# Making the two fp16 parts of a group's row maxima directly behind its last maxima

## The chip, the cores and the metric

The kernel runs on one core of a Trainium2 chip. The metric is the device time of one execution in microseconds (us). Engines are named as in the profile: PE is TensorE (matrix products and transposes), PEld its weight loads, DVE is VectorE, ACT is ScalarE, POOL is GpSimd, and SP is SyncE, which only issues DMAs here. Each engine takes its instructions in a fixed order and waits for the other engines by semaphores.

## The reference

Four layers work on a sequence of 2048 tokens of width 640, in the order A, B, A, B, each on the layer-normed stream and added back to it. A is linear attention with 32 heads of width 20. B is an attention in 4 segments of 512 tokens, with a memory of the segments before. The part that matters here is the softmax inside a segment of B:

```python
for s in range(N):                               # N = 4 segments, L = 512 tokens each
    qs, ks, vs = q[:, :, s], k[:, :, s], v[:, :, s]
    logits = einsum("bhqd,bhkd->bhqk", qs, ks) * scale + mask     # causal, 512 x 512 for each head
    p = softmax(logits, axis=-1)
    a_dot = einsum("bhqk,bhkd->bhqd", p, vs)
    a_mem = (phi(qs) @ M) / (phi(qs) @ z + 1e-6)
    o = g * a_mem + (1 - g) * a_dot
    M, z = M + phi(ks).T @ vs, z + phi(ks).sum()
```

## The kernel before

**Groups.** The 32 heads of a segment are done in 8 groups of 4 heads (two partition halves `par`, two heads `p` in each), so the two B layers have 2 x 4 x 8 = 64 groups. I number them 0 to 63 in the order of time. For each group the kernel does:

- `row_max`: the logits with the query rows on the partitions, 2 banks of PSUM per call (matmul L687); DVE reduces each block to the maximum of each query row under the causal mask (L694, a custom instruction that is followed by a read of its accumulator into a column of `mg`). A group has 16 of these, in five calls, `max` 0 to 4.
- The maxima as two fp16 rows: `m2` holds a high and a low part of `-mg / 2^14`, made by two DVE instructions (L703, L704) on 128 x 16 numbers. PE transposes `m2` (L707), ACT copies the 32 x 128 result out of PSUM (L709), and SP writes it by two small DMAs (L712) into the last rows of `qs`, so that the score matmul subtracts the maxima by itself.
- `scores`: the logits a second time, transposed (L724), exp on ACT (L728), the causal corner on POOL (L735).
- `weigh`: the weighted sum of `v` (L751, 16 steps in one bank), and `normalize`.

**The order of the work.** Two streams are woven together: the attention of one segment's groups, and the dense work of the next segment (projections L311 and L325, transposes L268, memory reads L370, output projections). The attention is given out in short bursts, three per group (`STRETCHES`), and dense work stands between the bursts. A burst works on three groups at once, written as "back" 0, 1 or 2: the new one, the one before, and the one before that. The first burst of a round holds the last scores of the oldest group, the first two calls of maxima of the new group, and then, for the group whose maxima were finished in the burst before, `rows`: `m2`, its transpose and the copies. The `sum` steps stand behind it.

**What sets each engine's order.** PE takes its instructions in the order in which the program was written (`MANUAL = ("PE",)`). For DVE, ACT, POOL and SP a scheduler orders the instructions: of those that it thinks ready it takes the one that was written first. So an instruction that is written later can be overtaken on DVE by others that are written earlier and are ready by then. All PSUM tiles share eight banks.

## Time and profile before

| | before |
|---|---|
| median of 3 runs | 1851.29 us (1851.12 to 1856.78) |
| the profiled execution | 1850.11 us, span 1848.4 us |
| PE busy | 1716.3 us, 93% of the span |
| DVE busy | 1144.3 us, 62% |
| ACT busy | 911.4 us, 49% |
| POOL busy | 503.3 us, 27% |
| granted PE clock, mean | 0.994 |
| L707, the transposes of `m2` | 64, of about 0.23 us |
| L703 and L704, the two parts | 64 each, of about 0.17 us |

The span is the time from the first to the last instruction of the profiled execution; the execution's own time is 1.7 us more. "Idle before" in brackets behind a row is how long the engine stood still ahead of that instruction, and behind the arrow is what ended the wait. The granted clock is 1.00 or 0.50 in any short stretch. Busy times of PE are spans of pipelined matmuls, so they say where PE was held up rather than how full it was. Where rows on one engine overlap, the next instruction has started before the last one's result was out.

### The profile page before, as it was taken

To read this page: it belongs to the slowest core of one execution; us is meant where nothing else is said; L and a number is where in the kernel's file an instruction comes from. 1 tells how busy PE (TensorE), PEld (TensorE's weight loads), DVE (VectorE), ACT (ScalarE), POOL (GpSimd) and SP (SyncE) were. 2 spreads that over 40 slices of the span, in tenths; PEclk is the share of its full clock that TensorE was granted. 3 is DMA by queue.
4 is the path that set the end of the run, shared out by engine and by line. 5 is a ranking of instruction groups with operands and counts; after the bars stand their busy time and mean duration, and the time that the engine had idled before them with its cause. 6 is when DMAs were issued, how large, how long until landed. Compare 5 with 4: busy or idle time off the path is not lost.

```text
span 1848.4 us, 36154 instructions
## 1 busy us (share of the span) xinstructions
PE 1716.3 (93%) x13032; PEld 1071.0 (58%) x13032; DVE 1144.3 (62%) x3890; ACT 911.4 (49%) x1696; POOL 503.3 (27%) x925
## 2 busy tenths in 40 slices
PE   6999999998999998898989999999989889898998
PEld 4666676654654565454556776756446546544555
DVE  7655353677767686766663421527677677677883
ACT  5455433266555545545554433333664665455553
POOL 1534430022122112224344334200221231232331
PEclk9999999999999999999999999999999999999999
DMA  7442443312222331351212112332122222223332
GB/s 253 157 183 89 158 151 107 107 52 88 78 65 87 109 98 59 112 192 65 70 55 86 51 33 92 133 115 90 55 86 91 85 90 89 94 76 105 121 111 87
DMA packets 123307, 185.96 MB, mean 101 GB/s; under 512 B 13676, under 2 KB 85484, under 8 KB 120952
## 3 DMA queue, kind: packets, MB, share of 16 engines
q1 hardware_dynamic: 109416, 137.44, 23.2%
q0 software_dynamic: 4496, 25.23, 3.8%
q10 hardware_dynamic: 9216, 20.98, 3.0%
q8 instruction: 103, 1.69, 0.4%
q14 instruction: 76, 0.62, 0.1%
HBM read 104.41 MB, written 78.64 MB: 99 GB/s over the span
## 4 chain that ended last, share of the span: by engine, by line
PE 73%; DVE 12%; ACT 6%; issue 4%; POOL 2%; DMA 2%; SPq 1%; POOLq 0%; ACTq 0%; DVEq 0%
PE ps L325 31%; PE ps L311 18%; PE ps L751 7%; DVE junk L694 5%; PE ps L268 4%; ACT pe L728 3%; PE ps L370 3%; PE ps L724 3%; PE ps L452 2%; PE ps L687 2%; POOL e L341 1%; PE ps L582 1%; PE ps L764 1%; DVE nat L547 1%; DVE st L286 1%
## 5 line engine op out<-in xcount | busy, mean ns | idle before, releaser
L694 DVE CUSTOM_DVE_ANT_0 junk<-ps,maskw 128x512 bf16<-128x512 f32 (+3 forms) x1024 | 499.3, 488 | 83.2 <-PE ps L687 27.0
L728 ACT ACTIVATE pe<-ps,lsc 128x512 f32<-128x512 f32 x640 | 392.6, 691 | 172.6 <-PE ps L724 170.6
L735 POOL TENSOR_SCALAR_AFFINE_SELECT pe<-pe 128x256 f32<-128x256 f32 (+1 forms) x640 | 234.2, 372 | 694.4 <-ACT pe L728 689.5
L325 PEld LDWEIGHTS <-xT 128*128 128x128 f16 x2880 | 281.8, 99 | 125.4 <-issue 19.4
L325 PEld LDWEIGHTS <-oT 128*128 128x128 f16 x1920 | 186.4, 98 | 78.7 <-issue 7.6
L341 POOL TENSOR_SCALAR e<-e 128x320 f32<-128x320 f32 (+1 forms) x104 | 163.8, 1575 | 163.2 <-ACT e L337 154.4
L751 PE MATMUL ps<-pe,v 128*32 128x512 f32 (+3 forms) x2048 | 159.4, 447 | 13.5 <-ACT pe L728 6.6
L724 PE MATMUL ps<-qs,ks 62*128 62x384 f16 (+3 forms) x1024 | 131.6, 299 | 33.8 <-DVE mg L694 22.8
L325 PE MATMUL ps<-w_Bv,xT 128*128 128x320 f16 x960 | 142.4, 302 | 1.9 <-DVE mg L694 1.9
L325 PE MATMUL ps<-w_Bo,oT 128*128 128x320 f16 x960 | 141.2, 299 | 2.6 <-DVE mg L694 1.4
L325 PE MATMUL ps<-w_Av,xT 128*128 128x320 f16 x960 | 140.8, 304 | 1.6 <-DVE w_Av L234 1.0
L311 PE MATMUL ps<-xT,w_Bq 128*128 128x512 f16 x600 | 139.5, 379 | 1.5 <-DVE mg L694 0.9
L311 PE MATMUL ps<-xT,w_Bk 128*128 128x512 f16 x600 | 139.5, 379 | 0.2 <-DVE xn L391 0.2
L325 PE MATMUL ps<-w_Ao,oT 128*128 128x320 f16 x960 | 139.5, 299 | 0.0
L311 PE MATMUL ps<-xT,w_Aq 128*128 128x512 f16 x600 | 136.0, 379 | 1.3 <-DVE xT L273 0.9
L325 PE MATMUL ps<-w_Ak,xT 128*128 128x320 f16 x960 | 135.6, 299 | 1.4 <-DVE mg L694 1.4
L348 ACT ACTIVATE v<-ps 128x320 f32<-128x320 f32 x128 | 55.5, 436 | 143.4 <-PE ps L325 139.1
L291 POOL TENSOR_TENSOR rs<-rs,mhalf 128x1 f32<-128x1 f32 x64 | 35.3, 552 | 302.7 <-DVE rs L290 302.4
L751 PEld LDWEIGHTS ps<-pe,v 128*32 128x32 f32 x2048 | 66.5, 112 | 82.8 <-issue 69.3
L687 PE MATMUL ps<-ks,qs 60*128 60x512 f16 (+3 forms) x1024 | 108.4, 297 | 5.5 <-ACT pe L728 3.4
L547 DVE SCALAR_TENSOR_TENSOR nat<-ps,nat 128x512 f16<-128x512 f32 x80 | 55.3, 691 | 89.9 <-ACT nat L546 87.5
L273 DVE TENSOR_TENSOR xT<-ps,xT 128x384 f16<-128x384 f32 (+1 forms) x128 | 60.3, 484 | 78.3 <-ACT xT L272 78.1
(151 smaller groups left out, 2228.5 us busy)
## 6 DMA issues: line engine op xcount, KB each, us to landing
x<-xn ACTq DMA_DIRECT2D x48, 320.0 KB
qs<-qd SPq DMA_DIRECT2D x128, 120.0 KB
ks<-kd SPq DMA_DIRECT2D x128, 120.0 KB
xo<-x SPq DMA_DIRECT2D x48, 320.0 KB
pqd<-pq POOLq DMA_DIRECT2D x40, 256.0 KB, 2.5
pqi<-pqd SPq DMA_DIRECT2D x32, 320.0 KB
qd<-nat SPq DMA_DIRECT2D x40, 256.0 KB
kd<-nat SPq DMA_DIRECT2D x40, 256.0 KB
```

The lines of the kernel that those rows point to most:

```text
L268: nc.tensor.transpose(pt[:, (c - c0) * P:(c - c0 + 1) * P], src[:, c * P:(c + 1) * P], self.ident)
L273: nc.vector.tensor_tensor(dst[:, c0:c1, 1, i * P:(i + 1) * P], v, hi, op=OP.subtract)
L311: nc.tensor.matmul(p, w[:, c, a, t * P:(t + 1) * P], xT[:, c, b, :], start=k == 0, stop=k == 3 * C - 1)
L325: nc.tensor.matmul(p, xT[:, c, a, i * P:(i + 1) * P], w[:, c, b, n * HN:(n + 1) * HN], start=k == 0, stop=k == 3 * C - 1)
L341: nc.gpsimd.tensor_scalar(e, e, 1.0, eps, op0=OP.min, op1=OP.add)
L547: nc.vector.scalar_tensor_tensor(nat[:, 1], p, QK_SHIFT, nat[:, 0], op0=OP.mult, op1=OP.subtract)
L687: nc.tensor.matmul(bs[par][:, a:a + n], qs[r, p, i * P:(i + 1) * P], ks[r, p, :n], start=True, stop=True)
L694: nc.vector.tensor_tensor_reduce(junk[:, :n], bs[par][:, a:a + n], self.maskw[:, SEG - n:], 1.0, NEG, OP.add, OP.max, G["mg"][:, par, p, i ...
L724: nc.tensor.matmul(b[:, a:a + n], ks[r, p, j * P:(j + 1) * P], qs[r, p, j * P:], start=True, stop=True)
L728: nc.scalar.activation(e, b, AF.Exp, scale=self.lsc)
L735: nc.gpsimd.affine_select(d, d, pattern=pat, compare_op=OP.is_ge, fill=0.0, base=0, channel_multiplier=-1)
L751: nc.tensor.matmul(G["pv"][32 * h4:32 * h4 + 32, j * P:], v[j][:, h * E1:h * E1 + 32], G.pop((p, par, j)), start=j == 0, stop=j == 2, skip ...
```

## The change

The two DVE instructions that make `m2` leave `max_rows` and get a method of their own, `split_max`. It is called from a new entry `split` in the third burst, directly behind the group's last call of maxima. The transpose, the copy and the two DMAs stay where they were, in the first burst of the next round, behind the first two calls of maxima of the next group. No instruction is added or removed.

```diff
-             [("exp", 2, 1), ("exp", 3, 1), ("max", 4, 0), ("load", 0, 0)]]
+             [("exp", 2, 1), ("exp", 3, 1), ("max", 4, 0), ("split", 0, 0), ("load", 0, 0)]]
...
-    def max_rows(self, G):
+    def split_max(self, G):
-        nc, bp, qs = self.nc, self.bp, G["qs"]
+        nc, bp = self.nc, self.bp
         mg = G["mg"].rearrange("q a p i -> q a (p i)")
         m2 = bp.tile([P, 2, 2, 2 * NT], F16, tag="m2", name="m2", bufs=2)
         nc.vector.tensor_scalar(m2[:, :, 0], mg, -1.0 / M_ONE, None, op0=OP.mult)
         nc.vector.scalar_tensor_tensor(m2[:, :, 1], mg, -1.0 / M_ONE, m2[:, :, 0],
                                        op0=OP.mult, op1=OP.subtract)
+        G["m2"] = m2
+
+    def max_rows(self, G):
+        nc, bp, qs, m2 = self.nc, self.bp, G["qs"], G.pop("m2")
         pt = self.ps.tile([P, 1024], F16, tag="ps", name="pm", bufs=8)
...
+                    elif op == "split":
+                        self.split_max(G)
```

In the new program L703 and L704 keep their line numbers; the transpose is L712, the copy L714, the two DMAs L717 and the score matmul L729.

PE's own order is the same, instruction by instruction. On DVE the two instructions stay in place in 50 of the 64 groups, because there they already stood directly behind the last maxima or behind one other instruction. They move in 14 groups. The first place is DVE's order at group 6, where the dense stream is in its memory reads (`oa`, `rc`, `acc`). `mg_4963` holds the maxima of group 6 and `mg_5193` those of group 7; each L694 with `junk` makes one maximum, and the L694 behind it reads it out. Before, from the first maxima of group 7 on:

```order
L694 ISA junk_5235,mg_5193<-ps_5231,maskw_76 128x512
L694 ISA mg_5193 128x1
L378 RECIPROCAL rc_5215<-rc_5215 128x16
L694 ISA junk_5237,mg_5193<-ps_5232,maskw_76 128x512
L694 ISA mg_5193 128x1
L381 TENSOR_TENSOR oa_5210<-ps_5211,rc_5215 128x320
L694 ISA junk_5245,mg_5193<-ps_5239,maskw_76 128x384
L694 ISA mg_5193 128x1
L703 TENSOR_SCALAR m2_5253<-mg_4963 128x2x8
L694 ISA junk_5247,mg_5193<-ps_5239,maskw_76 128x128
L694 ISA mg_5193 128x1
L704 SCALAR_TENSOR_TENSOR m2_5253<-mg_4963,m2_5253 128x2x8
```

Between the last maximum of group 6 and L704 stand four maxima of group 7 and five dense instructions (L381, L589 and L377 ahead of these rows). The same place after the change, where `mg_4966` is group 6 and `mg_5196` group 7, from the last maximum of group 6 on:

```order
L694 ISA mg_4966 128x1
L381 TENSOR_TENSOR oa_5124<-ps_5197,rc_5201 128x320
L703 TENSOR_SCALAR m2_5188<-mg_4966 128x2x8
L589 TENSOR_TENSOR acc_2749<-ps_5205,acc_2749 128x147
L704 SCALAR_TENSOR_TENSOR m2_5188<-mg_4966,m2_5188 128x2x8
L377 TENSOR_SCALAR rc_5218<-ps_5214 128x16
L694 ISA junk_5238,mg_5196<-ps_5234,maskw_76 128x512
L694 ISA mg_5196 128x1
```

The pair now stands ahead of all maxima of group 7, with L381 and L589 still ahead of L704. Group 38, the same place in the second B layer, reads alike. The second place is DVE's order at group 9, where `mv`, `rs`, `nb` and `xT` belong to the layer norm of the dense stream, `mg_5850` is group 9 and `mg_6210` group 10. Before, from behind the last maximum of group 9 on:

```order
L288 BN_AGGR mv_6219<-st_6216 128x2
L273 TENSOR_TENSOR xT_5523<-ps_6247,xT_5523 128x3x128
L290 TENSOR_SCALAR rs_6221<-mv_6219 128x1
L694 ISA junk_6269,mg_6210<-ps_6265,maskw_76 128x512
L694 ISA mg_6210 128x1
L293 TENSOR_SCALAR nb_6224<-mv_6219,rs_6221 128x1
L694 ISA junk_6271,mg_6210<-ps_6266,maskw_76 128x512
L694 ISA mg_6210 128x1
L703 TENSOR_SCALAR m2_6287<-mg_5850 128x2x8
L694 ISA junk_6279,mg_6210<-ps_6273,maskw_76 128x384
L694 ISA mg_6210 128x1
L704 SCALAR_TENSOR_TENSOR m2_6287<-mg_5850,m2_6287 128x2x8
```

The same place after the change, with `mg_5853` for group 9 and `mg_6213` for group 10:

```order
L288 BN_AGGR mv_6222<-st_6219 128x2
L273 TENSOR_TENSOR xT_5526<-ps_6250,xT_5526 128x3x128
L703 TENSOR_SCALAR m2_6205<-mg_5853 128x2x8
L290 TENSOR_SCALAR rs_6224<-mv_6222 128x1
L694 ISA junk_6272,mg_6213<-ps_6268,maskw_76 128x512
L694 ISA mg_6213 128x1
L704 SCALAR_TENSOR_TENSOR m2_6205<-mg_5853,m2_6205 128x2x8
L293 TENSOR_SCALAR nb_6227<-mv_6222,rs_6224 128x1
```

Of the three maxima of group 10 that stood ahead of L704, one still does, and L703 has none ahead of it. Group 17 reads alike. The third place is DVE's order at group 41, and group 49 reads as it does; `mg_17455` is group 41 and `mg_17815` group 42. Before:

```order
L286 BN_STATS st_17821<-xn_17730 128x6
L273 TENSOR_TENSOR xT_17128<-ps_17852,xT_17128 128x3x128
L288 BN_AGGR mv_17824<-st_17821 128x2
L694 ISA junk_17874,mg_17815<-ps_17870,maskw_76 128x512
L694 ISA mg_17815 128x1
L290 TENSOR_SCALAR rs_17826<-mv_17824 128x1
L703 TENSOR_SCALAR m2_17892<-mg_17455 128x2x8
L694 ISA junk_17876,mg_17815<-ps_17871,maskw_76 128x512
```

L704 follows five rows further down, behind a third maximum of group 42. After the change, with `mg_17458` for group 41:

```order
L286 BN_STATS st_17824<-xn_17730 128x6
L703 TENSOR_SCALAR m2_17810<-mg_17458 128x2x8
L273 TENSOR_TENSOR xT_17131<-ps_17855,xT_17131 128x3x128
L704 SCALAR_TENSOR_TENSOR m2_17810<-mg_17458,m2_17810 128x2x8
L288 BN_AGGR mv_17827<-st_17824 128x2
L694 ISA junk_17877,mg_17818<-ps_17873,maskw_76 128x512
```

Here both parts stand ahead of the maxima of the next group, with one transposed norm's evacuation (L273) between them.

In the other eight moved groups (8, 13, 16, 40, 45, 47, 48, 62) the pair passes one or two dense instructions, and at group 62 L704 also passes one maximum. Some PSUM tiles land in other banks, so that behind groups 6, 9, 17, 38, 41 and 49 PE's transposes L764 and some maxima L687 now name DVE among what they wait for. On SP the two copies of the maxima into `qs` now stand ahead of two loads of `qs` and `ks` at groups 6 and 38, and ahead of one such load and one load of `pqi` or `ol` at groups 41 and 49.

## The prediction

> I number the 64 groups of the two B layers in the order of time; "the pair" is L703 and L704, the two instructions that make `m2`.

> **What bounds the kernel now.** First the page: the span and the busy time of each engine.

> ```profile
> span 1848.4 us, 36154 instructions
> ...
> PE 1716.3 (93%) x13032; PEld 1071.0 (58%) x13032; DVE 1144.3 (62%) x3890; ACT 911.4 (49%) x1696; POOL 503.3 (27%) x925
> ```

> PE is busy for all but 1848.4 - 1716.3 = 132 us. It does the same work in the same order after the change, so all that can be won is idle time of PE and time at a low clock. Then the view of PE's waits over the whole span, and the same view for five stretches (450 to 540, 700 to 710, 1370 to 1450, 1590 to 1600 and 1790 to 1795 us). Columns: total us, how often, the longest.

> ```profile
> PE pm L707 <- DVE m L704: 22.4, 14, 3.7
> ```

> ```profile
> PE pm L707 <- DVE m L704: 5.8, 2, 3.1
> PE pm L707 <- DVE m L704: 3.1, 1, 3.1
> PE pm L707 <- DVE m L704: 5.6, 2, 2.9
> PE pm L707 <- DVE m L704: 3.7, 1, 3.7
> PE pm L707 <- DVE m L704: 0.9, 1, 0.9
> ```

> The reader is to see that the transposes wait for the pair for 22.4 us in all, and that it is a matter of few places: groups 6 and 9, 17, 38 and 41, 49 and 62 hold 5.8 + 3.1 + 5.6 + 3.7 + 0.9 = 19.1 us of it. These are groups at which the new order moves the pair. The other seven waits, 22.4 - 19.1 = 3.3 us, are short ones; there the pair already follows the last maxima or, at group 45, stays bound as shown below. They stay.

> **Why PE waits there.** DVE at group 9, in order of time (start, duration):

> ```profile
> 530.16 0.56 DVE L273 TENSOR_TENSOR xT<-ps,xT 128x384 f16<-128x384 f32 x1 [0.19 <-ACT xT L272]
> 530.63 0.14 DVE L290 TENSOR_SCALAR rs<-mv 128x1 f32<-128x1 f32 x1
> 530.69 0.68 DVE L694 CUSTOM_DVE_ANT_0 junk<-ps,maskw 128x512 bf16<-128x512 f32 x1
> 531.30 0.08 DVE L694 DVE_READ_ACCUMULATOR2_ANT mg<- 128x1 f32 x1
> ...
> 533.24 0.17 DVE L704 SCALAR_TENSOR_TENSOR m<-mg,m 128x16 f16<-128x16 f32 x1
> ```

> ```profile
> 533.46 0.23 PE L707 MATMUL pm<-ident,m 128*32 128x128 f16 x1 [3.10 <-DVE m L704]
> 533.57 3.45 PE L751 MATMUL ps<-pe,v 128*32 128x512 f32 x32
> ```

> PE was ready at 533.46 - 3.10 = 530.36. The pair is 0.34 us of work, but it stands behind maxima that belong to the next group. PE starts 0.05 us after L704 ends (533.24 + 0.17 to 533.46).

> **The change, place by place.** Nothing is added or removed; each sum says when L704 ends in the new order, from the rows' own starts and steps.

> Groups 9 and 17. L703 comes behind L273. L273's step to the next instruction was 530.63 - 530.16 = 0.47, so L703 starts at 530.63; it is of L704's kind and length, 0.17, and instructions here begin 0.05 to 0.08 before the one ahead has ended (L290 and L694 above), so I take 0.12 as its step; 0.17 is the upper bound. Then L290 (0.06 to the next), the first maximum with its read (530.69 to 531.30, 0.61), and L704 at about 531.42, ending at 531.59. PE starts at 531.64 instead of 533.46: 1.82 us won, of 3.10. With the upper bound for the step it is 1.77. Group 17 is the same piece of program, with the same wait (3.1): 1.82.

> Groups 6 and 38, the same view:

> ```profile
> 454.52 0.48 DVE L381 TENSOR_TENSOR oa<-ps,rc 128x320 f32<-128x320 f32 x1
> 454.93 0.30 DVE L589 TENSOR_TENSOR acc<-ps,acc 128x147 f32<-128x147 f32 x1
> 455.14 0.17 DVE L377 TENSOR_SCALAR rc<-ps 128x16 f32<-128x16 f32 x1
> ```

> ```profile
> 458.11 0.23 PE L707 MATMUL pm<-ident,m 128*32 128x128 f16 x1 [2.65 <-DVE m L704]
> 458.12 2.37 PE L751 MATMUL ps<-pe,v 128*32 128x512 f32 x32
> ```

> The new order is L381, L703, L589, L704. L703 starts at 454.93, L589 0.12 later, L704 0.21 behind that (455.14 - 454.93) at 455.26, and it ends at 455.43. PE was ready at 458.11 - 2.65 = 455.46 and starts at about 455.5: 2.6 us won, twice (the row of 1370 to 1450 holds 5.6 = 2.65 + 2.93 for groups 38 and 41).

> Groups 41 and 49, DVE behind the last maxima of each (from two stretches):

> ```profile
> 1444.02 0.49 DVE L286 BATCH_NORM_STATS2 st<-xn 128x6 f32<-128x320 f32 x1
> 1595.97 0.49 DVE L286 BATCH_NORM_STATS2 st<-xn 128x6 f32<-128x320 f32 x1
> 1596.38 0.54 DVE L273 TENSOR_TENSOR xT<-ps,xT 128x384 f16<-128x384 f32 x1
> 1596.83 0.20 DVE L288 BATCH_NORM_AGGREGATE mv<-st 128x2 f32<-128x12 f32 x1
> ```

> ```profile
> 1447.42 0.23 PE L707 MATMUL pm<-ident,m 128*32 128x128 f16 x1 [2.93 <-DVE m L704]
> 1599.64 0.29 PE L707 MATMUL pm<-ident,m 128*32 128x128 f16 x1 [3.73 <-DVE m L704]
> ```

> The new order is L286, L703, L273, L704. From L286's start: 0.41 + 0.12 + 0.45 (L273's step) + 0.17 + 0.05 = 1.20 us until PE starts. Group 41: 1444.02 + 1.20 = 1445.22 instead of 1447.42, 2.20 won. Group 49: 1597.17 instead of 1599.64, 2.47 won.

> Group 62: L704 passes the 0.61 us of a maximum; its wait is 0.9. I take 0.8, between 0.6 and 0.9. Group 45: the transpose's PSUM bank is now the one that L589 reads, and L589 stands behind L704 there, so PE waits for L589 in place of L704: 0, between -0.3 (L589's duration) and +0.3.

> Sum of the waits: 2 x 1.82 + 2 x 2.60 + 2.20 + 2.47 + 0.8 = 14.3 us. Bounds: all 19.1 us above, and 13.9 us with the steps at their upper bounds (0.05 us more in seven places).

> **The clock.** The view by stretches, cut at the times at which the granted clock changes (length, then busy us of PE, PEld, DVE, ACT, POOL, and the clock):

> ```profile
> 456.17:459.58 3.41, 1.47 (x17) 0.60 (x21) 2.75 (x13) 0.27 (x1) 0.16 (x1) 1.00 0.32 82
> 531.27:534.68 3.41, 1.22 (x13) 0.57 (x17) 2.77 (x15) 1.20 (x3) 0.85 (x2) 1.00 0.48 135
> 534.68:538.09 3.41, 3.41 (x29) 1.66 (x22) 0.02 (x2) 0.60 (x1) 0.00 (x0) 0.50 0.03 7
> 701.94:705.35 3.41, 0.90 (x9) 0.41 (x13) 2.80 (x13) 1.52 (x3) 1.18 (x3) 1.00 0.52 143
> 1596.23:1599.64 3.41, 0.00 (x0) 0.00 (x0) 3.04 (x14) 1.29 (x3) 1.36 (x3) 1.00 0.88 222
> ```

> After the wait of group 9 PE has half its clock for 3.41 us. The L751 row of group 9 tells it too: 3.45 us for the 32 products that take 2.37 at group 6. Stretches in which PE was busy for 0.00, 0.90 and 1.22 us are followed by such a one, the stretch with 1.47 is not. At half clock for 3.41 us PE loses up to 3.41 / 2 = 1.7 us; I take 1.6 of it, since not all steps there are clock-bound. With the waits cut to 1.3 us or less, the same stretches hold at least 3.41 - 1.3 = 2.1 us of PE work, above the 1.47 that kept the clock. So three drops go: 3 x 1.6 = 4.8 us more. Bounds: 0 (as many drops come elsewhere) and 5.1.

> [...]

> **Is the time given back later?** The maxima still have to be made, and PE now comes to the next burst up to 3.4 us (1.8 + 1.6) sooner at groups 9 and 17, 2.6 at 6 and 38, 2.2 at 41, 4.1 at 49. What could be late next is DVE. Its idle time ahead of the next thing that it waits for from PE, at groups 6, 9, 41 and 49:

> ```profile
> 463.30 0.18 DVE L377 TENSOR_SCALAR rc<-ps 128x16 f32<-128x16 f32 x1 [4.29 <-PE ps L370]
> 540.48 0.42 DVE L273 TENSOR_TENSOR xT<-ps,xT 128x256 f16<-128x256 f32 x1 [5.78 <-ACT xT L272]
> 1452.80 0.43 DVE L273 TENSOR_TENSOR xT<-ps,xT 128x256 f16<-128x256 f32 x1 [4.15 <-ACT xT L272]
> 1606.64 0.42 DVE L273 TENSOR_TENSOR xT<-ps,xT 128x256 f16<-128x256 f32 x1 [5.76 <-ACT xT L272]
> ```

> DVE clears its maxima and stands idle for 4.15 to 5.78 us at each place, more than what PE gains there by 1.6 us or more. So the cover holds, and I put the return at 0. If it were gone, up to all 19 us would come back as waits for maxima. What is queued behind the pair on DVE starts about 0.3 us later; none of it ends a wait of PE before that idle time. The copy L709 and its DMAs start with the transpose or when ACT is free, so they keep up.

> **The sum.** 14.3 + 4.8 = 19.1 us off the profiled execution's 1850.1, 1831.0 us. The median of the runs is 1.2 us above that execution: 1832.

> **The rivals.**

> 1. *The waits go, the clock does not follow.* The stretches lie on one grid (531.27 to 701.94 is 50 times 3.413 us, to 1596.23 it is 312 times), and the earlier PE comes, the further all later work moves against it; other idle times can then empty a stretch. Against it: a wait of 1.3 us cannot. [...] Price: 4.8 us; 1851.3 - 14.3 = 1837.
> 2. *The wait moves.* PE reaches the next burst sooner and stands there for PSUM banks that DVE still reads. For it speaks that PE's new waits name DVE at the transposes (L764) and maxima (L687) that follow group 6; against it the idle times of 4.15 us and more. If four fifths come back, 1851.3 - 0.2 x 19.1 = 1847.
> 3. *More than counted.* The short waits that stay (3.3 us) shrink too, or one more drop goes: 1832 - 5 = 1827.
> 4. *Slower: SP holds back the loads.* At groups 6, 38, 41 and 49 the two copies, which wait for ACT, now stand ahead of loads. SP at group 6, and the maxima for which those loads are the operands:

> ```profile
> 455.64 0.41 SPq L673 DMA_DIRECT2D ks<-kd  x1
> 458.67 1.30 SPq L712 DMA_DIRECT2D qs<-mt  x2
> ```

> ```profile
> 483.06 0.60 PE L687 MATMUL ps<-ks,qs 60*128 60x512 f16 x6
> ```

> The copies would leave at about 456.1 and the last load 1.3 us and more behind them, at about 457.8 instead of 455.6. They are read at 483.06 less what is won, some 22 us later. It decides only if a load takes over 22 us from issue to landing; then each of the four places loses what it is late by, and with 6 us at each it is 1832 + 24 = 1856.

> That the change does not do what it says cannot be for the seven places, since the new order of DVE shows the pair ahead.

> **How the numbers follow.** The forecast 1832, with its own range of 1829 to 1835: 0.62. Rival 1: 0.17. Rival 2: 0.11. Rival 3: 0.06. Rival 4: 0.04. The range is 1827 to 1842: it takes in the forecast, rivals 1 and 3 and the lower steps of 2, and leaves out about 0.15. A measurement of this kernel tells about 0.3%, 5.6 us, from no change. Faster than 1845.7: 0.62 + 0.17 + 0.06 and a little of rival 2, 0.87. Within: the rest of rival 2, 0.10. Slower: 0.03, most of rival 4.

> **What would show it.** In the new profile, PE's wait for L704 ahead of the transposes falls from 22.4 to about 8 us, with none above 1.4 us; the 32 products of L751 take 2.4 us at groups 9, 17 and 49; PE's busy time falls by some 5 us and its idle time by some 14; the waits of L724 and L687 for maxima stay as they are. If those waits grow by what L707 loses, rival 2 holds; if L751 at some group still takes over 3 us, rival 1; if PE waits for a DMA ahead of L687, rival 4. The forecast is wrong if the time is above 1842.

## The result and the profile after

| | before | after |
|---|---|---|
| median | 1853.19 us (1851.12 to 1856.78, 4 runs) | 1831.34 us (1829.49 to 1834.11, 4 runs) |
| the profiled execution | 1850.11 us | 1833.06 us |

The ratio is 0.9881, with a 95% interval of 0.9857 to 0.9905: the change makes the kernel 22 us faster. The profiled execution is 17.1 us shorter. The four runs of after lie at 1829.5, 1829.6, 1833.1 and 1834.1 us; the profiled one is the third of these.

The page of after, span and busy time of each engine:

```profile
span 1831.3 us, 36161 instructions
...
PE 1713.7 (94%) x13032; PEld 1070.3 (58%) x13032; DVE 1145.0 (63%) x3890; ACT 911.1 (50%) x1696; POOL 502.5 (27%) x925
```

PE's idle time, span less busy time, is 1831.3 - 1713.7 = 117.6 us, against 132.1 before: 14.5 us of the 17.1 are idle time that is gone, 2.6 us are busy time that is gone. The view of PE's waits of after (in us: the total, how often, the longest) tells where the idle time went. The transpose is now L712, the sums are L756 and the scores L729:

```profile
PE ps L729 <- DVE mg L694: 22.4, 42, 1.0
...
PE ps L756 <- ACT pe L733: 6.8, 17, 0.7
PE pm L712 <- DVE m L704: 6.0, 9, 1.2
...
PE ps L756 <- POOL rs L291: 3.2, 1, 3.2
...
PE pm L712 <- ACT r L339: 2.5, 7, 0.6
PE pm L712 <- DVE oT L273: 2.0, 3, 0.8
PE ps L756 <- DVE xn L391: 1.7, 3, 1.1
...
PE pm L712 <- ACT pe L733: 1.0, 1, 1.0
...
PE pm L712 <- DVE acc L589: 0.5, 1, 0.5
```

The wait for the pair fell from 22.4 us to 6.0, and its longest piece from 3.7 us to 1.2. The first row is the one to look at for a wait that merely moves: the scores wait 22.4 us for maxima, against 22.8 before. Nothing came back there. PE at groups 9, 49 and 6, in order of time (start and length):

```profile
529.48 0.23 PE L712 MATMUL pm<-ident,m 128*32 128x128 f16 x1 [1.24 <-DVE m L704]
529.58 2.36 PE L756 MATMUL ps<-pe,v 128*32 128x512 f32 x32
```

```profile
1583.41 0.23 PE L712 MATMUL pm<-ident,m 128*32 128x128 f16 x1 [0.96 <-ACT pe L733]
1583.51 2.36 PE L756 MATMUL ps<-pe,v 128*32 128x512 f32 x32
```

```profile
455.97 0.23 PE L712 MATMUL pm<-ident,m 128*32 128x128 f16 x1
```

Group 9 waits 1.24 us instead of 3.10, group 49 0.96 us instead of 3.73, and group 6 shows no wait behind its row, where it was 2.65. The 32 products of the sums take 2.36 us at groups 9 and 49, and at group 17 too, at full clock; before they took 3.45 us at group 9, 3.97 at 49 and 3.77 at 17. DVE at group 9 shows what the 1.24 us that are left consist of, and what is left of DVE's cover behind it:

```profile
528.51 0.17 DVE L703 TENSOR_SCALAR m<-mg 128x16 f16<-128x16 f32 x1
528.58 0.15 DVE L290 TENSOR_SCALAR rs<-mv 128x1 f32<-128x1 f32 x1
528.65 0.68 DVE L694 CUSTOM_DVE_ANT_0 junk<-ps,maskw 128x512 bf16<-128x512 f32 x1
...
529.25 0.17 DVE L704 SCALAR_TENSOR_TENSOR m<-mg,m 128x16 f16<-128x16 f32 x1
...
534.86 0.42 DVE L273 TENSOR_TENSOR xT<-ps,xT 128x256 f16<-128x256 f32 x1 [1.71 <-ACT xT L272]
```

One maximum of group 10 still stands between L703 and L704 (529.25 - 528.65 = 0.60 us). The last row is the idle time of DVE ahead of the next thing that it takes from PE's side: 1.71 us, where 5.78 stood before.

### The profile page after: what moved, and what is told of

Same layout as the page of the kernel before. It is cut to its first block, busy times and chain, and to the rows that moved or that the text cites. A ratio compares the mean times of both kernels' runs of the same rounds, so it can differ in the third digit from the quotient of the medians.

```text
span 1831.3 us, 36161 instructions
## 1 busy us (share of the span) xinstructions
PE 1713.7 (94%) x13032; PEld 1070.3 (58%) x13032; DVE 1145.0 (63%) x3890; ACT 911.1 (50%) x1696; POOL 502.5 (27%) x925
## 4 chain that ended last, share of the span: by engine, by line
PE 75%; DVE 11%; ACT 6%; issue 4%; POOL 2%; DMA 2%; SPq 1%; POOLq 0%; ACTq 0%; DVEq 0%
PE ps L325 33%; PE ps L311 18%; PE ps L756 7%; DVE junk L694 4%; PE ps L268 4%; ACT pe L733 3%; PE ps L370 3%; PE ps L729 3%; PE ps L452 2%; PE ps L687 2%; POOL e L341 1%; PE ps L582 1%; PE ps L769 1%; DVE nat L547 1%; PE ps L574 1%
## 5 line engine op out<-in xcount | busy, mean ns | idle before, releaser
L694 DVE CUSTOM_DVE_ANT_0 junk<-ps,maskw 128x512 bf16<-128x512 f32 (+3 forms) x1024 | 499.5, 488 | 83.2 <-PE ps L687 27.1
L756 PE MATMUL ps<-pe,v 128*32 128x512 f32 (+3 forms) x2048 | 155.4, 438 | 13.7 <-ACT pe L733 6.8
L729 PE MATMUL ps<-qs,ks 62*128 62x384 f16 (+3 forms) x1024 | 132.2, 299 | 33.4 <-DVE mg L694 22.4
L687 PE MATMUL ps<-ks,qs 60*128 60x512 f16 (+3 forms) x1024 | 108.4, 297 | 5.8 <-ACT pe L733 3.6
L756 PEld LDWEIGHTS ps<-pe,v 128*32 128x32 f32 x2048 | 65.3, 110 | 81.2 <-issue 66.3
L546 ACT ACTIVATE nat<-ps 128x512 f16<-128x512 f32 x80 | 48.0, 600 | 105.9 <-PE ps L311 76.3
```

Of the source, the lines that this page charges most:

```text
L687: nc.tensor.matmul(bs[par][:, a:a + n], qs[r, p, i * P:(i + 1) * P], ks[r, p, :n], start=True, stop=True)
L694: nc.vector.tensor_tensor_reduce(junk[:, :n], bs[par][:, a:a + n], self.maskw[:, SEG - n:], 1.0, NEG, OP.add, OP.max, G["mg"][:, par, p, i ...
L729: nc.tensor.matmul(b[:, a:a + n], ks[r, p, j * P:(j + 1) * P], qs[r, p, j * P:], start=True, stop=True)
L756: nc.tensor.matmul(G["pv"][32 * h4:32 * h4 + 32, j * P:], v[j][:, h * E1:h * E1 + 32], G.pop((p, par, j)), start=j == 0, stop=j == 2, skip ...
```

## The experiments

Each is told with the median of its runs and the ratio to the kernel before on the same chip.

### The two halves of the gain

The pair is made early at three groups only, those whose waits were followed by half clock (9, 17, 49); then at four others only (6, 38, 41, 62). Elsewhere it stays where it was before.

```diff
+EARLY = (9, 17, 49)              # the second kernel: (6, 38, 41, 62)
...
     def max_rows(self, G):
 
+        if "m2" not in G:
+            self.split_max(G)
...
                     elif op == "split":
+                        if G["id"] in EARLY:
+                            self.split_max(G)
```

> The pair is made early at groups 9, 17 and 49 alone, the three places behind which the clock was halved; all other groups keep the order of before (DVE's order differs from before at these three groups and nowhere else). My theory (waits and clock add up place by place): the waits of the transposes fall by 1.9 + 1.9 + 2.8 = 6.5 us, from 22.4 to about 16, and with them go the clock drops behind them, 0 to 4.8 us: 1841 to 1846 against some 1852 for the kernel before. Rival A (the gain comes from the other places or from the new bank places): no change, 1852. Rival B (the clock is all that matters): 1832 to 1836.

> The pair is made early at groups 6, 38, 41 and 62 alone, where no clock drop followed. My theory: the waits fall by 2.6 + 2.6 + 2.2 + 0.9 = 8.3 us, from 22.4 to about 14, and the drops behind groups 9, 17 and 49 stay: about 1844 against some 1852. Rival B (only the clock counts): no change, 1852. The two runs together should give what the change gives, about 20 us, if the places do not act on each other.

Measured: 1842.56 us for groups 9, 17 and 49, ratio 0.9946 (0.9928 to 0.9964), and 1840.85 us for the four others, ratio 0.9943 (0.992 to 0.9965). The page and the waits of the first (its transpose is L715, the second part of the pair L705):

```profile
span 1836.3 us, 36161 instructions
...
PE 1710.4 (93%) x13032; PEld 1067.8 (58%) x13032; DVE 1144.5 (62%) x3890; ACT 910.0 (50%) x1696; POOL 501.7 (27%) x925
```

```profile
PE pm L715 <- DVE m L705: 16.1, 14, 2.9
```

The waits of the second:

```profile
PE pm L715 <- DVE m L705: 13.2, 11, 3.1
```

In the first, PE's idle time falls by 132.1 - (1836.3 - 1710.4) = 6.2 us and its busy time by 1716.3 - 1710.4 = 5.9 us. The terms of the prediction for these groups are 2 x 1.82 + 2.47 = 6.1 us of waits and 4.8 us of clock. In the second (span 1839.5 us, PE busy 1715.8) idle time falls by 8.4 us and busy time by 0.5; the terms are 2 x 2.60 + 2.20 + 0.8 = 8.2 us and none. So the waits come out as the prediction has them, place by place. The clock's part does not belong to three groups alone, though. Behind groups 9, 17 and 49 the first kernel keeps the full clock, but that its 5.9 us come so near to 4.8 is luck: three more of the seven half-clock stretches of before are gone in it, and three new ones have come, two of them behind group 6. There the wait is the same 2.65 us as before, and the 32 products now take 4.55 us instead of 2.37:

```profile
456.17 4.55 PE L759 MATMUL ps<-pe,v 128*32 128x512 f32 x32
```

In the second kernel the clock still drops behind groups 9 and 17, but not behind 49, where the wait is 3.01 us; one more stretch, at 90 us, makes up for it. Its time, 1840.85 us, is some 3 us below the 1844 that was expected with no part for the clock. The two halves by their ratios, 10.0 and 10.6 us, add up to the change's 22 within their intervals.

### The clock by itself

The kernel before, with the pair in its old place, and ten products ahead of the transpose at six groups. They write numbers that nothing reads into the transpose's own bank, and only keep PE at work during the wait.

```diff
         pt = self.ps.tile([P, 1024], F16, tag="ps", name="pm", bufs=8)
+        if G["id"] in FILL:              # FILL = (6, 9, 17, 38, 41, 49)
+            for _ in range(10):
+                nc.tensor.matmul(pt.bitcast(F32)[:, :512], self.blk[:, :P], self.blk[:, :512],
+                                 start=True, stop=True)
```

> The kernel before, with ten extra matrix products (128x128 by 128x512, into the transpose's own bank, which overwrites them) in front of the transpose at groups 6, 9, 17, 38, 41 and 49. DVE's order is that of before. The products run while PE would stand idle, so they cost nothing by themselves. If the halved clock costs 1.6 us at each of three places, the time falls by up to 4.8 us, to about 1847, while the pair still comes as late as before (PE's idle time ahead of the transposes is only filled). If the clock after a wait does not matter: no change, 1852.

Measured: 1847.73 us, ratio 0.9979 (0.9965 to 0.9992): faster, by 1.5 to 6.5 us, with more work in it. PE at group 9 (the added products are L710, of which nine are in the trace; the transpose is L711, the sums L755), and the wait in all:

```profile
528.66 2.33 PE L710 MATMUL pm<-blk 128*128 128x512 bf16 x9
531.83 0.23 PE L711 MATMUL pm<-ident,m 128*32 128x128 f16 x1 [0.83 <-DVE m L705]
531.93 2.36 PE L755 MATMUL ps<-pe,v 128*32 128x512 f32 x32
```

```profile
PE pm L711 <- DVE m L705: 8.5, 14, 1.2
...
PE pm L711 <- DVE nat L547: 4.7, 1, 4.7
```

At group 9 the added products (2.33 us) and the wait that is left (0.83) fill the 3.10 us of the old wait: no time is won there. But the sums behind them take 2.36 us, not 3.45. Half clock is granted in 2 stretches of 3.41 us, against 7 before (the end of the span left out). The clock is thus a cost of its own. The span is only 1848.4 - 1843.1 = 5.3 us shorter with five stretches fewer, since the second row of waits, 4.7 us once, is one that the kernel before does not have. It stands at group 23, where nothing was added, and goes back to ACT, which waits there 5.3 us for one DMA that writes `nat` out.

What one stretch costs is told better by the runs. The kernel before ran 38 times beside the other kernels of this part, with mean granted clocks of 0.986 to 0.994 (1 is full clock from end to end) and times of 1863.9 to 1846.2 us. A straight line through them gives 1.5 us for each 0.001 of the clock. As 0.001 of the clock is 0.001 x 1853 x 2 / 3.41 = 1.1 stretches, one stretch costs about 1.4 us; that is an estimate from these runs. With it the mean clocks give each kernel's gain by the clock:

| kernel | runs | mean granted clock | kernel before | gain by the clock, estimated |
|---|---|---|---|---|
| the change | 4 | 0.9953 | 0.9910 (38 runs) | 6.4 us |
| early at 9, 17, 49 | 10 | 0.9938 | 0.9912 (19 runs) | 3.9 us |
| early at 6, 38, 41, 62 | 4 | 0.9933 | 0.9912 (19 runs) | 3.1 us |
| filled waits | 10 | 0.9963 | 0.9912 (19 runs) | 7.7 us |

Both halves gain by the clock, and about alike. The one profile of before shows half clock behind three of the long waits; the profiles of the two halves show it behind others (group 6) and not behind all of these (group 49), and the mean clock of one kernel differs from run to run. The kernel with filled waits gains most by the clock, but only 5 us in all between the medians; where the rest of its 7.7 goes is open.

### How much cover is left

Extra instructions on DVE, of about 0.7 us each, whose results nothing reads, stand behind the first maxima of the next group at six places: two of them at each, then seven.

```diff
+    def pad(self, G, new):
+        if G["id"] not in PADDED:        # PADDED = (6, 9, 17, 38, 41, 49)
+            return
+        v = G["st"]["v"][0][:, :SEG]
+        for _ in range(PAD):                 # 2, then 7
+            junk = self.bp.tile([P, SEG], BF16, tag="junk", name="junk", bufs=1)
+            self.nc.vector.scalar_tensor_tensor(junk, v, new["mg"][:, 1, 0, 0:1], v,
+                                                op0=OP.mult, op1=OP.add)
```

> The changed kernel, with two extra DVE instructions (128x512 in 32 bits, about 0.65 us each, 1.3 us together; their result is not used) behind the first maxima of the next group at groups 6, 9, 17, 38, 41 and 49. This tests whether DVE's idle time there, 1.46 to 1.83 us in the profile after, is free cover. My theory: no change, 1831 (at most 1 us more). Rival 2 of the prediction in its mild form (the gain is already close to being given back to DVE): up to 6 x 1.3 = 8 us more, 1839.

> The same with seven such instructions, about 4.5 us at each of the six places, 27 us of DVE work in all. My theory: the first 1.5 to 1.8 us at each place are hidden, and DVE's second idle stretch of 1.5 us behind it at groups 9, 17, 41 and 49 hides as much again; the rest comes out as waits of PE for maxima: 4 x 1.2 + 2 x 3.0 = 11 us, 1842 (1838 to 1848). If DVE were not a limit there at all: 1831.

Measured: with two 1831.41 us, ratio 0.9857 (0.9825 to 0.9888), which is the time of the change; with seven 1847.06 us, ratio 0.9954 (0.9936 to 0.9971). The pages' rows of the two:

```profile
PE 1714.4 (93%) x13032; PEld 1070.9 (58%) x13032; DVE 1153.5 (63%) x3902; ACT 911.2 (50%) x1696; POOL 502.0 (27%) x925
```

```profile
PE 1715.6 (93%) x13032; PEld 1071.5 (58%) x13032; DVE 1173.1 (64%) x3932; ACT 911.8 (50%) x1696; POOL 504.1 (27%) x925
```

DVE has 8.5 us more to do in the first, 28.1 us more in the second (1145.0 in after). The first costs nothing. Of the second's 28.1 us about half comes out in the time: 13.5 us against the ratio of the change (0.9954 and 0.9881 of 1853 us), 15.7 us between the medians of these two kernels, which ran on one chip, and 9.8 us between the profiled spans (1841.1 against 1831.3). Some 5 us of the 15.7 are clock, by the estimate above (0.9924 against 0.9960 in the mean of the runs). PE behind group 9, where the scores (L738) now wait for a maximum:

```profile
542.34 0.37 PE L738 MATMUL ps<-qs,ks 62*128 62x512 f16 x1 [2.02 <-DVE mg L695]
```

The scores have no wait for maxima at this place in after. In all, their waits for maxima grow by 3.5 us (25.9 against 22.4), not by the 11 of the expectation, and their waits for the exponentials on ACT by 4.3 (5.3 against 1.0), which the expectation did not have. So the cover of DVE is what keeps the gain, and it has an end between 8.5 / 6 = 1.4 us and 28.1 / 6 = 4.7 us at each place. The 1.71 us of the DVE row above lie within it.

### Another place for the transpose

The waits that the change leaves at the transpose could be hidden by work that stands ahead of it. The changed kernel, with the transpose, its copy and the DMAs behind the first `sum` step, and then behind two:

```diff
-STRETCHES = [[("exp", 4, 2), ("max", 0, 0), ("max", 1, 0), ("rows", 0, 1), ("sum", 0, 2), ("sum", 1, 2), ("sum", 3, 2),
+STRETCHES = [[("exp", 4, 2), ("max", 0, 0), ("max", 1, 0), ("sum", 0, 2), ("rows", 0, 1), ("sum", 1, 2), ("sum", 3, 2),
```

> The changed kernel, with transpose, copy and DMAs behind the first step of the weighted sum (0.6 us of PE work later); the pair stays directly behind the last maxima. My theory: the waits that are left at the transposes (6.0 us for the pair, 2.5 for ACT, 2.5 for DVE's evacuations) shrink by up to 0.6 us each, about 6 us in all: 1825 against 1831 for the changed kernel. Rival C (the rows land too late for the scores): no better than 1831.

> The same, behind the first two steps of the weighted sum (1.2 us later). My theory: nearly all of the waits that are left at the transposes go, 8 to 10 us: 1822 to 1824. Rival C: the scores of the groups with the least room between the copies and the scores wait for the DMA, and some or all of it is lost: 1826 to 1835.

The kernel before with the same places of `rows`, which here holds the pair too; first behind two steps, later behind one:

> The kernel before, with the whole of max_rows (pair, transpose, copy, DMAs) behind the first two steps of the weighted sum instead of ahead of them: PE has 1.2 us of other work to do while the pair comes. DVE's order of the pair is that of before. My theory (only PE's idle time at the transpose counts, whoever hides it): each of the six large waits shrinks by 1.2 us (7.2 in all), the short ones (3.3 us, and 4.5 us of waits for ACT and PSUM banks) mostly go: 12 to 16 us less, 1836 to 1840. Rival C (the rows then land too late for the scores): the scores of most groups wait for the DMA and the time does not fall, 1850 or more.

> The kernel before, with the pair, its transpose, copy and copies to qs written behind the first sum step (the kernel that beat the change has the same place for the transpose, but the pair early). It completes a square: pair early or not, transpose ahead of or behind the first sum step. Theory (both count, and the pair's lateness is shortened by the step that now stands ahead of the transpose): the step takes about 1.1 us of PE, so of the long waits of before (3.1 at groups 9 and 17, 2.65 and some 2.9 at 6 and 38, 2.93 at 41, 3.73 at 49) about 1.2 us each are covered, 18 - 7 = 11 us stay, and with up to three clock drops of 1.6 us the time is 1813 + 11 to 16 = 1824 to 1829 us; PE's wait for the pair at the transpose is 8 to 12 us in all. Rival A (only the place of the transpose counts, the pair's place is no matter then): about 1813 us, wait for the pair under 2 us. Rival B (the pair, which is now written behind the step too, gets later on DVE by what PE gains, nothing is covered): 1813 + 18 + 5 = 1836 us, wait for the pair about 18 us.

Measured:

| pair | transpose ahead of the sums | behind the first step | behind the second |
|---|---|---|---|
| in `rows`, as before | 1 (the kernel before) | 0.9877 (0.9841 to 0.9912), 1829.32 us | 0.9852 (0.9833 to 0.987), 1824.88 us |
| early, the change | 0.9881 (0.9857 to 0.9905), 1831.34 us | 0.976 (0.9731 to 0.9788), 1812.86 us | 0.9795 (0.9769 to 0.9821), 1819.44 us |

The best is the pair early and the transpose behind the first step: 1812.86 us (1808.93 to 1814.96), faster than both kernels. The two edits of the first two columns add up within the intervals: 0.9881 x 0.9877 = 0.976. With two steps they do not: 0.9881 x 0.9852 = 0.9735, and 0.9795 was measured. Three of the four expectations gave too long a time: 1825 for this one, 1822 to 1824 for two steps, 1836 to 1840 for the kernel before with two steps. They counted only the waits at the transpose itself. The page and the waits of the best kernel (transpose L711, sums L755):

```profile
span 1813.2 us, 36160 instructions
...
PE 1707.3 (94%) x13032; PEld 1065.4 (59%) x13032; DVE 1143.8 (63%) x3890; ACT 915.1 (50%) x1696; POOL 501.7 (28%) x925
```

```profile
PE ps L755 <- POOL pe L739: 4.4, 5, 1.2
...
PE ps L755 <- ACT r L338: 3.1, 7, 0.7
...
PE pm L711 <- ACT r L338: 2.2, 1, 2.2
...
PE pm L711 <- DVE oT L272: 1.6, 2, 0.8
...
PE pm L711 <- DVE m L703: 0.5, 2, 0.2
```

Idle time is 105.9 us, 11.7 less than in after, and busy time 6.4 less. The transposes waited 12.0 us by the rows of after (6.0 + 2.5 + 2.0 + 1.0 + 0.5) and wait 4.3 by these; the sums waited 11.7 us (6.8 + 3.2 + 1.7) and wait 7.5. With the smaller rows of both views, which are not shown, the transposes go from 12.0 to 4.5 us and the sums from 13.4 to 8.9. The expectation had only the transposes' waits. It missed the sums' (4.5 us less, above all the 17 waits for `pe`) and the 6.4 us of busy time, which are not the clock, since both profiles have five stretches at half clock ahead of their end. Group 60 shows one piece of program in both; in after, PE only:

```profile
1749.02 0.60 PE L687 MATMUL ps<-ks,qs 60*128 60x512 f16 x6
1749.61 0.23 PE L712 MATMUL pm<-ident,m 128*32 128x128 f16 x1
1750.16 2.36 PE L756 MATMUL ps<-pe,v 128*32 128x512 f32 x32 [0.32 <-DVE xn L391]
1752.46 0.55 PE L268 MATMUL ps<-ident,ol 128*128 128x128 f32 x3
```

and in the best kernel, PE and one weight load:

```profile
1732.19 0.60 PE L686 MATMUL ps<-ks,qs 60*128 60x512 f16 x6
1732.72 1.07 PE L755 MATMUL ps<-pe,v 128*32 128x512 f32 x8
1733.61 0.22 PE L711 MATMUL pm<-ident,m 128*32 128x128 f16 x1
1733.61 1.51 PE L755 MATMUL ps<-pe,v 128*32 128x384 f32 x24
1735.05 0.55 PE L267 MATMUL ps<-ident,ol 128*128 128x128 f32 x3
```

```profile
1733.18 0.10 PEld L711 LDWEIGHTS <-m 128*32 128x32 f16 x1 [0.30 <-DVE xn L390]
```

From the maxima's start to the next dense product it is 3.44 us in after and 2.86 here, 0.58 less, at a group where the pair was never late. 0.32 of it is a wait of the sums for `xn`, an instruction that reads a PSUM bank. In the best kernel the same instruction ends an idle time of the transpose's weight load (0.30 us), and the eight products of the first step cover it. So the wait for `xn` has passed from the sums to the transpose, which now has work ahead of it. What makes it pass is not shown, since no kernel here changes the bank alone. The rest, about 0.25 us, is the transpose's own time, which now lies inside the run of the sums (its row and the second row of the sums both start at 1733.61). Added over the 64 groups, this piece of PE's program is 18.8 us shorter than in after, by the start times in the two traces; the spans differ by 18.1. It is spread unevenly: 31 groups gain 0.25 to 0.94 us each, the others less.

Where the pair is not early, the step ahead of the transpose covers only a part of its lateness. The waits of the kernel before with `rows` behind the first step:

```profile
PE pm L707 <- DVE m L704: 11.8, 6, 2.4
```

That is inside the 8 to 12 us that the theory gave, and far from both rivals (2 and 18 us). Its time, 1829.32 us, lies just above 1824 to 1829 us; its profile also has a wait of 5.1 us at group 23, where ACT waits for a DMA of `nat` as in the kernel with filled waits. With the pair early, one step is better than two: the two kernels ran on one chip, and their runs do not overlap (1808.93 to 1814.96 and 1817.28 to 1819.65 us). Of the 6.6 us between the medians some 4 are clock, by the estimate above (0.9965 against 0.9938). The waits do not tell the rest: with two steps the scores' wait for the copies of the maxima grows from 3.7 to 7.0 us, and their wait for maxima falls from 24.9 to 21.5.

## Why the prediction was right

**The waits** (14.3 us): right, to the size of a row. The idle time that went is 14.5 us. Group by group: 1.24 us are left at groups 9 and 17, so 1.86 each were won (1.82 in the prediction, which took 0.12 us from L703 to the next instruction, where the rows of after show 528.58 - 528.51 = 0.07); 0.09 at 6, 2.56 won (2.60); 0.70 at 41, 2.23 won (2.20); 0.96 at 49, which the view puts down to ACT and not to the pair, 2.77 won (2.47); 0 at 62, 0.9 won (0.8); 0.48 at group 45, credited to `acc` as said, nothing won. The forecast for the wait for L704, about 8 us with nothing above 1.4, came out at 6.0 and 1.24.

**The clock** (4.8 us): that shorter waits keep the clock was right; which drops, and how many, was not. The term was three drops of 1.6 us, read from one execution. In the profiled pair the three behind groups 9, 17 and 49 went, but a new one came at 1716.51 us: of 7 stretches at half clock 5 are left, and busy time fell by 2.6 us, 1.3 for each of the two. The step that does not hold is the limit, that more than 1.47 us of PE work in a stretch keeps the clock; a row of before already speaks against it (last section). The lower bound (as many come elsewhere) and rival 1 had named drops elsewhere, and in this pair that came true for one drop in three. Over the runs the term was too small instead: 0.9953 against 0.9910 of granted clock is 4.7 stretches fewer, about 6.4 us at the estimated 1.4 for each. The first kernel of the two halves shows why one pair of profiles cannot give the count: the unchanged wait of group 6 lost the clock there and kept it before.

**The return** (0): right. The scores' wait for maxima is 22.4 us (22.8 before). The cover of 4.15 to 5.78 us shrank to 1.46 at group 6, 1.71 at 9, 1.83 at 41 and 1.82 at 49, where the prediction had 1.6 us or more left over. The two kernels with extra DVE work show that it is this cover that decides: 1.4 us more at each place cost nothing, 4.7 us more gave back 13.5 of 22 us. Rival 2 was a real mechanism, a few us of DVE work away.

**SP and the loads** (rival 4): it did not come to pass. The waits of L687 in after name ACT and DVE and no load, and the scores wait 1.5 us for the copies of the maxima (2.4 before).

**The sum**: 1832 against 1831.34 us. That it is so near is in part luck. The profiled pair differs by 17.1 us instead of 19.1, the clock's term being 2.2 too large there, while the medians differ by 21.9, and the median before rose from 1851.29 to 1853.19 us with its fourth run. Waits of 14.5 us and a clock of about 6.4 come near the medians. What the prediction left out was a prize about as large beside it: with the transpose ahead of the sums, its own 0.23 us and the wait behind it stay in PE's way at about half of the groups, 18.5 us between the two medians.

## What to carry to other kernels

Where a tiny instruction on a busy engine feeds the bound engine, write it directly behind its producer: a scheduler that takes what was written first lets all that is written ahead of it go first, here the maxima of the next group. The gain is what the trace shows between producer and consumer in the new order, and it stays only as long as the engine has idle time ahead of its next due time, so read that idle time as a budget: here 1.4 us more at each place cost nothing, and 4.7 us more gave back 13.5 of 22 us. And look at what stands between the waiting instruction and long work that is ready: here one step of such work ahead of the transpose took the wait for the pair from 22.4 to 11.8 us by itself, and the ratios of the two edits, 0.9881 and 0.9877, multiply to the 0.976 that both together gave.

## What the runs showed of the hardware

The prediction held that a stretch of 3.41 us with more than 1.47 us of PE work keeps the clock. Two rows of before that the prediction does not show already say otherwise: a stretch with 2.08 us of PE work is followed by one at half clock (length, then busy us of PE, PEld, DVE, ACT, POOL, and the clock):

```profile
1282.20:1285.61 3.41, 2.08 (x16) 0.96 (x16) 2.98 (x13) 2.12 (x4) 0.85 (x2) 1.00 0.08 25
1285.61:1289.02 3.41, 3.41 (x15) 1.99 (x14) 3.32 (x11) 1.76 (x4) 0.89 (x3) 0.50 0.26 99
```

The same view of after:

```profile
528.70:532.11 3.41, 2.63 (x35) 1.31 (x36) 2.41 (x11) 1.59 (x4) 1.33 (x3) 1.00 0.56 144
...
1272.78:1276.19 3.41, 2.07 (x15) 0.69 (x14) 3.06 (x15) 1.72 (x3) 0.70 (x2) 1.00 0.20 59
1276.19:1279.60 3.41, 3.41 (x15) 2.28 (x15) 3.28 (x10) 2.16 (x5) 1.02 (x4) 0.50 0.20 78
...
1713.10:1716.51 3.41, 2.28 (x16) 0.88 (x15) 3.14 (x15) 3.32 (x7) 1.90 (x5) 1.00 0.02 5
1716.51:1719.92 3.41, 3.38 (x13) 1.93 (x13) 2.13 (x10) 1.69 (x3) 1.63 (x4) 0.50 0.01 2
```

```profile
451.24:454.65 3.41, 2.15 (x17) 1.14 (x15) 3.23 (x13) 2.66 (x5) 1.62 (x4) 1.00 0.43 126
454.65:458.07 3.42, 1.91 (x13) 0.70 (x17) 2.32 (x13) 0.27 (x1) 0.00 (x0) 0.50 0.24 57
```

The kernel with filled waits shows the practical side: unused products in waits that were left in place were worth 1.5 to 6.5 us, at a mean granted clock of 0.9963 against 0.9912.
